# A recurrent attention kernel: small SBUF buffers laid out anew, and the score mask issued after the turn of q

## The chip, the cores and the metric

The kernel runs on one core of one Trainium2 chip. The metric is the device time of one execution in microseconds; three runs of the kernel before gave 2310.14, 2313.74 and 2330.06 us, so the median is 2313.74 us. Core engines are named as in the profile: PE (TensorE, matmuls; PEld is its weight load), DVE (VectorE), ACT (ScalarE), POOL (GpSimd) and SP (SyncE, which here only issues transfers). "L807" is line 807 of the kernel.

## The reference

Two branches work on the same 2048 tokens of width 1024 and are mixed by a sigmoid gate. The feed-forward branch is `gelu(x @ w_gate) * (x @ w_up) @ w_down`. The attention branch is a recurrence over 64 segments of 32 tokens; 8 memory rows go from each segment to the next:

```python
for s in range(n_seg):
    h = concatenate([mem, x[:, 32*s : 32*s+32]])      # 40 rows
    q, k, v = h @ Wq, h @ Wk, h @ Wv                  # 32 heads of 128
    scores = q k^T * scale, masked where idx >= M and key > query
    o = softmax(scores) v
    o = einsum('bhte,hed->btd', o, Wo)
    mem = o[:, :8]
    outs.append(o[:, 8:])
```

The next segment can't begin before `o[:, :8]` is there, and every segment needs all four weight matrices of 8 MB each, which don't all fit into SBUF.

## The kernel before, in words

**The rows.** Each segment is 40 rows: 8 of memory and 32 tokens. Only 24 of the tokens and the 8 memory rows (32 rows) go through the products with the fresh `h` (tile hT, [128, 8, 32], two of them, taken by turns: hT0 for even segments, hT1 for odd ones). The other 8 tokens of a segment don't depend on the memory as inputs, so their q, k and v are made ahead for four segments at once, from hR. This is called a fill (L836): eight products into one PSUM bank, a copy by ACT into a staging tile (fill_evac, L860), and for q and k a transpose on PE, a copy by DVE in place and a store to the DRAM scratch qk_scr (fill_put, L871); v is stored straight to v_scr. They are loaded back a segment at a time into qkr (load_qk, L542) and vB (load_v, L548).

**A segment.** The heads are taken in two halves, u = 0 and 1; r = 0 is the half that a segment does first (r = u exclusive-or the parity of s). Each of the products k, q, v and o is eight pieces (n = 0 to 7) for each half, four matmuls of 32 output rows on the four column groups of the array per piece. `walk` (L330) writes the order out: k 0 to 3, q 0 and 1 (r = 0), the last four pieces of the previous segment's o (r = 1), q 2 and 3, v 0 to 3, k 4 to 7, q 4 to 7, v 4 to 7; then k, q (r = 1), o (r = 0), v (r = 1), and o 0 to 3 (r = 1). All else is hung into this order by `plan` (L903): `on(m, r, n, f)` runs f just before piece n of product m. So each engine's instruction order is the order in which plan and walk emit; engines run in that order, and waits come from the overlap of SBUF byte ranges (cells of 64 bytes) and PSUM banks that `_Prog` (L31) records.

**Steps that the change touches.** With k in a PSUM bank, ACT copies it to a staging tile (evac, L671), PE turns it (four 128x128 transposes, L678), DVE copies it into kT (trans, L685), and POOL adds the 8 made-ahead columns from qkr (put_rest, L882). q goes the same way into qT. scores (L694) is one PE operation: first a matmul that writes the mask into bank SS (L697), then 32 small matmuls that add the scores (L703); DVE and ACT make the softmax, which ends in tAB (L723, over qT's memory). attend (L725) multiplies with vA and vB; take (L750) copies the result to oT; rest_o (L756) has POOL gather the 8 made-ahead rows into oRc, which SP stores to o_scr (L985), for a product over all segments at the end. After the first four pieces of o (r = 1), fold (L815) adds two halves of the output on DVE (with a scratch tile, part, in between) into a_bf; next_mem (L822) turns the memory rows out of a_bf into the next hT. fold and next_mem come twice, for the two halves of the width. POOL stores a_bf to a_scr (L1003).

**Weights.** 50 slots in SBUF hold the pieces; most have a slot of their own, while pieces 0 and 1 of k and q, 0 to 4 of v and 0, 1, 4, 5 and 6 of o share a slot between the halves and are loaded anew in each segment, about 7 MB. SP issues each of these loads when PE is through with the piece that it overwrites (spent, L447); neighbours are joined into one load of 1 MB (load_two, L425). All loads by SP go through one queue (q1), hT's (load_h, L533) among them.

**Memory of the small buffers.** In order of address, with bytes per partition: hT0 512, vB 512, hT1 512, qkr 768, oRc 512, a_bf 512, kT 1280, qT 1024, oT 1280. Others lie over these: part (1024, two of them by turns) over the old hT and vB; vA over oT; the staging tiles kS over kT, qS over qT, oS over oT, and pS over oRc and a_bf. kS takes Wk's first half and a segment's first fill, oS the second fill (two of every four segments have two fills), pS Wk's second half.

Of the kernel before, what the change touches and what calls it, by code (L numbers as in the profile page):

```python
# [210 lines left out]
def bass_gated_mix__memory_aug_recurrent_mem_tr__geglu_ffn__prompt_kernel(  # L211
# [34 lines left out]
    with ExitStack() as es:  # L246
# [57 lines left out]
        assert a_bf.off == oRc.off + 512  # L304
        stage = {n: al(n + "S", [128, 512], at=t.off) for n, t in (("k", kT), ("q", qT), ("o", oT), ("p", oRc))}
# [360 lines left out]
        def dve_copy(o, i, rd, wr):  # L666
            op("dve", lambda e: e.tensor_copy(o, i), rd=rd, wr=wr)  # L667
# [26 lines left out]
        def scores(u):  # L694

            def f(e):
                e.matmul(PB[SS][:, 0:320].rearrange("p (a c) -> p a c", a=4), lhsT=ident[:, :],  # L697
                         rhs=mS[:, :].unsqueeze(1).to_broadcast([128, 4, 80]), start=True, stop=False, skip_group_check=True)
                for n, c in ((32, 0), (8, 40)):
                    for j in range(4):  # L700
                        for g in range(4):
                            x = 8 * (4 * j + g)
                            ins = e.matmul(PB[SS][32 * g:32 * g + n, j * 80 + c:j * 80 + c + LQ],  # L703
                                           lhsT=qT[:, j, g, :] if n == 32 else qkr[:, 2 * u, x:x + 8],
                                           rhs=kT[:, j, g, :], start=False, stop=True, skip_group_check=True)
                return ins
            op("pe", f, rd=[qT.r(), qkr.r(256 * u, 256 * u + 128), kT.r(), ident.r(), mS.r()], wr=[BK(SS)])
# [107 lines left out]
        def fold(s, b):  # L815
            lo, hi = slice(64 * b, 64 * b + 64), slice(64 - 64 * b, 128 - 64 * b)
            pt, cs = part[s % 2], slice(256 * b, 256 * b + 256)
            op("dve", lambda e: e.tensor_copy(pt[lo, :], PB[XO][hi, cs]), rd=[BK(XO)], wr=[pt.r()])  # L818
            op("dve", lambda e: e.tensor_tensor(out=a_bf[lo, :], in0=PB[XO][lo, cs], in1=pt[lo, :], op=ALU.add),
               rd=[BK(XO), pt.r()], wr=[a_bf.r()])  # L820
# [82 lines left out]
        def plan(s):  # L903
# [29 lines left out]
            if not last:  # L933
                on("k", 0, 4, lambda: load_h(s + 1))
# [9 lines left out]
            if s > 0:  # L944
                on("v", 0, 7, lambda: scores(ua))
# [3 lines left out]
            if s == 0:  # L949
                on("k", 1, 1, lambda: scores(ua))  # L950
                on("k", 1, 1, lambda: attend(ua))
                on("k", 1, 1, lambda: fill0("k", 1, B0, "k"))
                on("q", 1, 0, lambda: fill0("q", 1, B1, "q"))
                on("q", 1, 4, lambda: fill0("v", 1, B2, "k"))
                on("q", 1, 4, lambda: (load_qk(0, 1), load_v(0, slice(1, 2)), load_r(1) if NG > 1 else None))
            else:
                on("v", 0, 5, lambda: load_qk(s, 1))
            on(*(("q", 1, 1) if s else ("o", 0, 0)), lambda: evac(bank_of["k", 1], stage["p" if s else "k"], "act"))
            if s > 0:
                on("o", 0, 0, lambda: attend(ua, ((0, "dve"),), TT))  # L960
                on("o", 0, 0, lambda: evac(bank_of["q", 1], stage["q"], "act"))
                on("o", 0, 0, lambda: trans(kT, "p", A0))
                on("o", 0, 0, lambda: put_rest())
                on("o", 0, 0, lambda: take(((1, "act"), (2, "act"))))
                on("o", 0, 2, lambda: trans(qT, "q", SS))
                on("o", 0, 2, lambda: take(((3, "dve"),), TT))
                on("o", 0, 2, lambda: rest_o(ua))
                on("o", 0, 4, lambda: scores(ub))
            else:
                on("o", 0, 0, lambda: trans(kT, "k"))  # L970
                on("o", 0, 0, lambda: put_rest())
                on("o", 0, 0, lambda: evac(bank_of["q", 1], stage["q"], "act"))
                on("o", 0, 2, lambda: trans(qT, "q"))
                on("o", 0, 6, lambda: scores(ub))
# [38 lines left out]
        fold(NSEG - 1, 1)  # L1013
# [4 lines left out]
        for b in range(NBK):  # L1018
            rb = rbs[b % 2]
            for hf in range(2):  # L1020
# [9 lines left out]
                cp[("act", "dve")[hf]](rb[0:RB, hf * 512:hf * 512 + 512], PB[bk][0:RB, :], [BK(bk)], [rb.r(hf * 512, hf * 512 + 512)])  # L1030
# [143 lines left out]
```

## Time and profile before

| what | number |
|---|---|
| median of three runs | 2313.74 us |
| the profiled execution itself | 2317.11 us |
| its span, first to last instruction | 2315.3 us |
| mean granted TensorE clock | 0.986 |
| PE busy | 2130.5 us (92%) |
| DVE, ACT, POOL busy | 1028.5, 543.2, 433.0 us |
| moved by DMA | 638.35 MB, mean 276 GB/s |
| of it by SP's queue (q1) | 596.59 MB |

Busy times say how much of the span an engine worked. A wait names the engine or transfer that released an instruction and the idle time ahead of it; idle time of an engine counts only where it sets the end. The ends of matmuls are modelled, so where PE seems busy the distance from start to start tells more. For a transfer the profile gives the issue and the time to landing, in which waiting in the queue is counted. Segments stand in the trace as stretches between stores of oRc (SPq L985). The recurrence takes the span up to about 1665 us, the rest is the product for the made-ahead rows and the feed-forward branch.

### The profile page before, as it was taken

The page shows a single profiled execution, that of the slowest core. Times are in us where ns is not written, and L with a number is a line of the kernel's source. Part 1 is how long each engine was busy: PE and PEld are TensorE (multiplying, and loading weights), DVE is VectorE, ACT ScalarE, POOL GpSimd, SP SyncE. Part 2 cuts the span into 40 slices and gives each one's busy share as a digit, 9 for nine tenths or more (in the row PEclk, how much of TensorE's full clock was granted, in tenths as well). Part 3 has the DMA queues.
Part 4 walks back from the last instruction along what each step waited for, and adds up shares of the span by engine and source line. Part 5 has one row for each costly group of instructions (what it writes and reads, how often), then busy time and mean ns, then how long its engine had stood idle before and what let it go on. Part 6 is the DMA issues. An engine that isn't in the chain of part 4 may idle for free.

```text
span 2315.3 us, 74604 instructions
## 1 busy us (share of the span) xinstructions
PE 2130.5 (92%) x33852; PEld 1060.6 (46%) x33852; DVE 1028.5 (44%) x2440; ACT 543.2 (23%) x1111; POOL 433.0 (19%) x821
## 2 busy tenths in 40 slices
PE   4488999999999999999999999998899999999999
PEld 2244444444444444444454445444464444444444
DVE  3344444444444444444444444444315346163462
ACT  1122222222222222222222222222113123032130
POOL 4422222222222222222222222221100000000000
PEclk9799999999999999999999999999999999999999
DMA  9999999899898999989999899998964450803520
GB/s 373 353 306 333 333 338 348 305 337 333 314 336 319 328 340 324 345 323 334 347 327 349 310 335 345 320 331 319 340 201 159 137 163 10 285 25 117 178 88 19
DMA packets 251964, 638.35 MB, mean 276 GB/s; under 512 B 23256, under 2 KB 92120, under 8 KB 251648
## 3 DMA queue, kind: packets, MB, share of 16 engines
q1 hardware_dynamic: 227824, 596.59, 72.3%
q0 software_dynamic: 13888, 26.31, 3.8%
q10 hardware_dynamic: 9936, 10.69, 1.4%
q8 instruction: 266, 4.36, 0.7%
q14 instruction: 50, 0.41, 0.1%
HBM read 596.85 MB, written 36.63 MB: 274 GB/s over the span
## 4 chain that ended last, share of the span: by engine, by line
PE 66%; DMA 22%; DVE 4%; issue 4%; ACT 3%; POOL 1%; ACTq 0%; POOLq 0%; SPq 0%
PE pb L774 19%; PE pb L1075 15%; DMA sl<-in_A_Wv_dram 7%; PE pb L1129 5%; PE pb L807 5%; PE pb L844 5%; DMA qk_scr<-oS 4%; PE pb L790 4%; PE pb L681 3%; PE pb L1026 3%; PE pb L854 2%; DMA qkr<-qk_scr 2%; PE pb L1110 2%; DMA wall<-wo_scr 1%; DMA xr_scr<-xr 1%
## 5 line engine op out<-in xcount | busy, mean ns | idle before, releaser
L774 PE MATMUL pb<-sl,hT 128*32 128x512 bf16 x12288 | 771.9, 382 | 27.0 <-issue 19.4
L774 PEld LDWEIGHTS pb<-sl,hT 128*32 128x32 bf16 x12288 | 348.7, 97 | 310.5 <-issue 37.6
L844 PE MATMUL pb<-sl,hR 128*32 128x512 bf16 x3072 | 221.3, 390 | 2.4 <-issue 1.8
L1075 PE MATMUL pb<-xT,wg 128*128 128x512 bf16 x896 | 211.7, 379 | 0.7
L1075 PE MATMUL pb<-xT,wu 128*128 128x512 bf16 x896 | 211.7, 379 | 0.0
L807 PE MATMUL pb<-wall,oT 128*32 128x256 bf16 x4056 | 148.7, 274 | 17.8 <-DMA wall<-in_A_Wo_dram 7.0
L757 POOL COPY oRc<-oT 128x128 bf16<-128x128 bf16 x128 | 96.3, 752 | 361.7 <-DVE oT L667 360.2
L790 PE MATMUL pb<-wall,oT 128*32 128x512 bf16 x2048 | 153.2, 391 | 9.5 <-issue 6.2
L818 DVE COPY part<-pb 64x256 f32<-64x256 f32 x128 | 54.0, 422 | 235.3 <-PE pb L807 234.3
L664 ACT ACTIVATE kS<-pb 128x512 bf16<-128x512 f32 x127 | 75.8, 597 | 344.2 <-PE pb L774 322.4
L1129 PE MATMUL pb<-wd,GT 128*128 128x512 bf16 x672 | 146.3, 379 | 1.3 <-DMA wd<-in_B_w_down_dram 1.3
L711 ACT ACTIVATE E<-pb 128x320 bf16<-128x320 f32 x128 | 56.0, 438 | 371.6 <-DVE pb L710 371.6
L1083 ACT ACTIVATE s<-pb 128x512 f32<-128x512 f32 x112 | 66.8, 596 | 311.7 <-PE pb L1075 311.7
L1075 PEld LDWEIGHTS pb<-xT,wg 128*128 128x128 bf16 x896 | 87.2, 98 | 107.9 <-DVE GT L1091 3.7
L1075 PEld LDWEIGHTS pb<-xT,wu 128*128 128x128 bf16 x896 | 87.7, 98 | 105.7
L1084 DVE SCALAR_TENSOR_TENSOR tp<-s,pb 128x512 f32<-128x512 f32 x112 | 76.9, 687 | 124.2 <-ACT s L1083 124.0
L807 PEld LDWEIGHTS pb<-wall,oT 128*32 128x32 bf16 x4056 | 100.3, 96 | 67.6 <-ACT oT L664 26.1
L667 DVE CAST oT<-pb 128x160 bf16<-128x160 f32 x256 | 76.4, 320 | 115.2 <-PE pb L740 115.2
L667 DVE COPY kT<-pb 128x512 bf16<-128x512 bf16 x128 | 54.4, 425 | 158.1 <-PE pb L681 157.7
L664 ACT ACTIVATE vA<-pb 128x512 bf16<-128x512 f32 x128 | 76.2, 596 | 199.1 <-PE pb L774 151.7
L883 POOL COPY kT<-qkr 128x128 bf16<-128x128 bf16 x128 | 37.3, 292 | 431.2 <-DVE kT L667 272.5
L1088 DVE SCALAR_TENSOR_TENSOR tp<-tp,pb 128x512 f32<-128x512 f32 x112 | 77.0, 687 | 78.5 <-ACT tp L1087 78.5
(93 smaller groups left out, 2283.1 us busy)
## 6 DMA issues: line engine op xcount, KB each, us to landing
sl<-in_A_Wv_dram SPq DMA_DIRECT2D x128, 1024.0 KB, 11.2
wall<-wo_scr SPq DMA_DIRECT2D x175, 512.0 KB, 6.3
sl<-in_A_Wk_dram SPq DMA_DIRECT2D x64, 1024.0 KB, 5.8
sl<-in_A_Wq_dram SPq DMA_DIRECT2D x64, 1024.0 KB, 9.3
wall<-wo_scr SPq DMA_DIRECT2D x55, 1024.0 KB, 8.4
wd<-in_B_w_down_dram SPq DMA_DIRECT2D x42, 1024.0 KB, 5.6
sl<-in_A_Wv_dram SPq DMA_DIRECT2D x75, 512.0 KB, 11.6
wall<-in_A_Wo_dram SPq DMA_DIRECT2D x41, 512.0 KB, 7.7
```

The costliest lines, as they stand in the source:

```text
L664: op("act", lambda e: e.activation(o, i, ACTF.Copy), rd=rd, wr=wr)
L667: op("dve", lambda e: e.tensor_copy(o, i), rd=rd, wr=wr)
L681: ins = e.transpose(PBV[bank][:, j * 128:(j + 1) * 128], st[:, j * 128:(j + 1) * 128], ident[:, :])
L757: op("pool", lambda e: e.tensor_copy(oRc[:, :, 16 * u:16 * u + 16].rearrange("p c x -> p x c"), oT[:, :, :, 32:40].rearrange("p g j c -> p ...
L774: ins = e.matmul(PB[bk][32 * g:32 * g + 32, :], lhsT=h[:, i, :], rhs=w[:, g * 512:(g + 1) * 512], start=(n == 0), stop=(n == 7))
L790: ins = e.matmul(PB[XO][32 * g:32 * g + 32, :], lhsT=oT[:, j, x, 0:32], rhs=wall[:, na:nb + 1:nb - na, c:c + 256], start=(n == 0 and hp == 0),
L807: ins = e.matmul(PB[XO][32 * g:32 * g + 32, 256 * b:256 * b + 256], lhsT=oT[:, j, x, 0:32], rhs=w[:, c:c + 256], start=False, stop=(n % 4 ...
L844: ins = e.matmul(PB[b][32 * g:32 * g + 32, :], lhsT=h[:, k[2], :], rhs=w[:, g * 512:(g + 1) * 512], start=(n == 0), stop=(n == 7))
L1075: ins = e.matmul(PB[bk][:, 0:FB], lhsT=w[:, kc, cc:cc + 128], rhs=xT[:, :, :, kc, :].rearrange("p t i c -> p (t i) c"), start=(kc == 0), s ...
L1084: op("dve", lambda e, hg=hg, t=t: e.scalar_tensor_tensor(out=t[:, :], in0=s1[:, :], scalar=1.0, in1=hg, op0=ALU.add, op1=ALU.mult), rd=[BK ...
L1088: op("dve", lambda e, hu=hu, t=t: e.scalar_tensor_tensor(out=t[:, :], in0=t[:, :], scalar=1.0, in1=hu, op0=ALU.add, op1=ALU.mult), rd=[BK( ...
L1129: ins = e.matmul(PB[bank[2 * k + hf]][:, :], lhsT=GT[:, j, tb * 128:(tb + 1) * 128], rhs=w[:, jj, hf * 512:(hf + 1) * 512], start=(j == 0) ...
```

## The change

The layout becomes hT0, oRc, hT1, qkr, vB, a_bf, kT, qT, oT. part is one tile over qT. Two staging tiles of 1024 bytes replace pS and the use of oS in the recurrence: stage 0 is hT0 and oRc, stage 1 is oRc and hT1. In segment s the fill's second store and Wk's second half both use the stage with the hT of the previous segment. So load_h(s + 1), which writes that hT, moves from before k 4 to after the turn of Wk's second half at o 0 (r = 0). fill_evac of the second fill moves from before q 2 to the end of the steps at k 0, fill_put from before v 3 to before q 2 (behind fold). load_v moves from behind fold(s, 1) to before o 2 (r = 1). The mask matmul becomes an operation of its own, issued right after the turn of q; the second q's turn uses bank A1 instead of SS, so that SS is free for the mask. `ended` adds one wait in the last product, since part now lies where that product's result is copied.

```diff
         hT0 = al("hT0", [128, KC, 32])
+        oRc = al("oRc", [128, NB, 32])
+        hT1 = al("hT1", [128, KC, 32])
+        assert oRc.off == hT0.off + 512 and hT1.off == oRc.off + 512
+        hT = (hT0, hT1)
+        qkr = al("qkr", [128, 3, 128])
         vB = al("vB", [128, 2, 128])
-        hT1 = al("hT1", [128, KC, 32])
-        assert vB.off == hT0.off + 512 and hT1.off == vB.off + 512
-        hT = (hT0, hT1)
-        part = tuple(al(f"part{n}", [128, 256], FP32, at=o) for n, o in enumerate((hT0.off, vB.off)))
-        qkr = al("qkr", [128, 3, 128])
-        oRc = al("oRc", [128, NB, 32])
         a_bf = al("a_bf", [128, 256])
...
-        assert a_bf.off == oRc.off + 512
-        stage = {n: al(n + "S", [128, 512], at=t.off) for n, t in (("k", kT), ("q", qT), ("o", oT), ("p", oRc))}
+        part = al("part", [128, 256], FP32, at=qT.off)
+        stage = {n: al(f"{n}S", [128, 512], at=t.off) for n, t in (("k", kT), ("q", qT), ("o", oT), (0, hT0), (1, oRc))}
...
-        def scores(u):
+        def mask():
+            op("pe", lambda e: e.matmul(PB[SS][:, 0:320].rearrange("p (a c) -> p a c", a=4), lhsT=ident[:, :],
+                                        rhs=mS[:, :].unsqueeze(1).to_broadcast([128, 4, 80]), start=True, stop=False,
+                                        skip_group_check=True), rd=[ident.r(), mS.r()], wr=[BK(SS)])
+
+        def scores(u, masked=True):
+            if not masked:
+                mask()
...
-            if not last:
+            if not last and s == 0:
                 on("k", 0, 4, lambda: load_h(s + 1))
...
             on("v", 0, 5 if s else 6, lambda: trans(qT, "q", A0 if s else TT))
             if s > 0:
+                on("v", 0, 5, mask)
                 on("v", 0, 7, lambda: scores(ua))
...
-            on(*(("q", 1, 1) if s else ("o", 0, 0)), lambda: evac(bank_of["k", 1], stage["p" if s else "k"], "act"))
+            on(*(("q", 1, 1) if s else ("o", 0, 0)), lambda: evac(bank_of["k", 1], stage[ub if s else "k"], "act"))
             if s > 0:
                 on("o", 0, 0, lambda: attend(ua, ((0, "dve"),), TT))
                 on("o", 0, 0, lambda: evac(bank_of["q", 1], stage["q"], "act"))
-                on("o", 0, 0, lambda: trans(kT, "p", A0))
+                on("o", 0, 0, lambda: trans(kT, ub, A0))
+                if not last:
+                    on("o", 0, 0, lambda: load_h(s + 1))
                 on("o", 0, 0, lambda: put_rest())
                 on("o", 0, 0, lambda: take(((1, "act"), (2, "act"))))
-                on("o", 0, 2, lambda: trans(qT, "q", SS))
+                on("o", 0, 2, lambda: trans(qT, "q", A1))
+                on("o", 0, 2, mask)
                 on("o", 0, 2, lambda: take(((3, "dve"),), TT))
                 on("o", 0, 2, lambda: rest_o(ua))
                 on("o", 0, 4, lambda: scores(ub))
...
             if two:
-                on("q", 0, 2, lambda: fill_evac(*fl[1], B0, "o"), **nx)
+                on("k", 0, 0, lambda: fill_evac(*fl[1], B0, ua), **nx)
             on("q", 0, 2, lambda: fold(s, 1), **nx)
-            on("q", 0, 2, lambda: load_v(s + 1), **nx)
+            if two:
+                on("q", 0, 2, lambda: fill_put(*fl[1], ua, SS), **nx)
+            on("o", 1, 2, lambda: load_v(s + 1))
             on("v", 0, 3, lambda: next_mem(s, 1), **nx)
-            if two:
-                on("v", 0, 3, lambda: fill_put(*fl[1], "o", SS), **nx)
...
-                cp[("act", "dve")[hf]](rb[0:RB, hf * 512:hf * 512 + 512], PB[bk][0:RB, :], [BK(bk)], [rb.r(hf * 512, hf * 512 + 512)])
+                cp[("act", "dve")[hf]](rb[0:RB, hf * 512:hf * 512 + 512], PB[bk][0:RB, :], [BK(bk)], [rb.r(hf * 512, hf * 512 + 512)],
+                                       *([[ended]] if hf and b < 2 else []))
```

More of the change, by code (lines that the diff above doesn't have):

```diff
@@ L664, in act_copy, with dve_copy @@
             op("act", lambda e: e.activation(o, i, ACTF.Copy), rd=rd, wr=wr)
-        def dve_copy(o, i, rd, wr):
-            op("dve", lambda e: e.tensor_copy(o, i), rd=rd, wr=wr)
+        def dve_copy(o, i, rd, wr, after=()):
+            op("dve", lambda e: e.tensor_copy(o, i), rd=rd, wr=wr, after=after)
         cp = {"act": act_copy, "dve": dve_copy}
@@ L706, in f @@
                 return ins
-            op("pe", f, rd=[qT.r(), qkr.r(256 * u, 256 * u + 128), kT.r(), ident.r(), mS.r()], wr=[BK(SS)])
+            op("pe", f, rd=[qT.r(), qkr.r(256 * u, 256 * u + 128), kT.r()], wr=[BK(SS)])
             op("pool", lambda e: e.memset(pAB[:, 256:544].bitcast(FP32), 0.0), wr=[pAB.r(256)])
@@ L816, in fold @@
             lo, hi = slice(64 * b, 64 * b + 64), slice(64 - 64 * b, 128 - 64 * b)
-            pt, cs = part[s % 2], slice(256 * b, 256 * b + 256)
+            pt, cs = part, slice(256 * b, 256 * b + 256)
             op("dve", lambda e: e.tensor_copy(pt[lo, :], PB[XO][hi, cs]), rd=[BK(XO)], wr=[pt.r()])
-            op("dve", lambda e: e.tensor_tensor(out=a_bf[lo, :], in0=PB[XO][lo, cs], in1=pt[lo, :], op=ALU.add),
+            return op("dve", lambda e: e.tensor_tensor(out=a_bf[lo, :], in0=PB[XO][lo, cs], in1=pt[lo, :], op=ALU.add),
                rd=[BK(XO), pt.r()], wr=[a_bf.r()])
@@ L949, in plan @@
             if s == 0:
-                on("k", 1, 1, lambda: scores(ua))
+                on("k", 1, 1, lambda: scores(ua, False))
                 on("k", 1, 1, lambda: attend(ua))
@@ L973, in plan @@
                 on("o", 0, 2, lambda: trans(qT, "q"))
-                on("o", 0, 6, lambda: scores(ub))
+                on("o", 0, 6, lambda: scores(ub, False))
             on("v", 1, 0, some(f1, 3))
@@ L1012, in bass_gated_mix__memory_aug_recurrent_mem_tr__geglu_ffn__prompt_kernel @@
         fold(NSEG - 1, 0)
-        fold(NSEG - 1, 1)
+        ended = fold(NSEG - 1, 1)
         op("pool", lambda e: e.dma_start(a_scr[NSEG - 1].rearrange("g r c -> (g r) c"), a_bf[:, :]), rd=[a_bf.r()],
```

2 lines of the change are left out of this document (removed).

## The prediction

> **What bounds the kernel now.** I read the page first (TensorE 92% busy, DMA at nine tenths), then the sums by stage, because the recurrence and the feed-forward part have different limits, then the waits, then the order of time of one segment.
>
> ```profile
> 1000.00:1300.00 300.00, 285.86 (x6086) 147.37 (x6086) 144.14 (x396) 78.22 (x174) 77.05 (x154) 1.00 0.94 340
> 1014.73:1039.07 24.34, 23.18 (x497) 12.02 (x498) 11.72 (x32) 6.43 (x14) 5.68 (x11) 1.00 0.93 332
> 1700.00:2315.30 615.30, 610.26 (x2847) 283.36 (x2845) 275.69 (x405) 139.18 (x227) 0.00 (x0) 1.00 0.38 122
> ```
>
> The columns are the stretch, its length, busy PE, PEld, DVE, ACT, POOL, the granted clock, the DMA share and GB/s. The change lies wholly in the recurrence (about 90 to 1665 us, 64 segments of some 24.3 us; the second row is one of them, from one store of oRc to the next). There PE is busy 95% of the time and the DMA engines 93 to 94%: two resources near their limit at once, so a wait that goes on one side is worth only what the other side lets through. The last 615 us are untouched.
>
> ```profile
> ACT vA L664 <- DMA qk_scr<-oS: 47.4, 24, 2.9
> PE pb L732 <- ACT vA L664: 17.3, 24, 1.5
> PEld pb L774 <- DMA sl<-in_A_Wv_dram: 20.2, 31, 1.8
> PEld pb L697 <- DVE qT L667: 53.1, 112, 0.9
> PE pb L697 <- POOL kT L883: 6.9, 9, 1.1
> PEld pb L681 <- ACT pS L664: 10.1, 32, 1.3
> ```
>
> Each row of the waits: who waited, for what, total us, times, longest. The first two are the stall that the new layout is about: half of the segments store a second fill from oS, which is oT's and vA's memory, so vA's copy waits for that store and PE's attend (L732) waits for vA. The third names the other limit: in 31 segments PE's weights for the last Wv pieces come only just from the DMA.
>
> ```profile
> 1022.20 0.77 POOL L879 DMA_DIRECT2D qk_scr<-oS  x1 [0.57 <-DVE oS L876]
> 1029.68 0.60 ACT L664 ACTIVATE vA<-pb 128x512 bf16<-128x512 f32 x1 [2.17 <-PE pb L774]
> 1030.17 0.59 ACT L664 ACTIVATE pS<-pb 128x512 bf16<-128x512 f32 x1
> 1030.33 0.27 PE L732 MATMUL pb<-tAB,vA 32*128 32x40 bf16 x16 [0.73 <-ACT vA L664]
> 1030.82 0.40 PE L681 MATMUL pb<-ident,pS 128*128 128x128 bf16 x4
> 1082.85 0.40 PE L774 MATMUL pb<-sl,hT 128*32 128x512 bf16 x4 [0.29 <-DMA sl<-in_A_Wv_dram]
> ```
>
> Here is the one kind of segment (PE idle 0.73 us for vA at 1030) and the other (PE idle for Wv at 1082).
>
> ```profile
> 1017.98 0.38 SPq L436 DMA_DIRECT2D sl<-in_A_Wk_dram  x1
> 1022.23 0.49 SPq L535 DMA_DIRECT2D hT<-xq_scr  x1
> 1024.20 0.34 SPq L381 DMA_DIRECT2D sl<-in_A_Wv_dram  x1
> sl<-in_A_Wv_dram SPq DMA_DIRECT2D x75, 512.0 KB, 11.6
> hT<-xq_scr SPq DMA_DIRECT2D x63, 64.0 KB, 12.2
> vB<-v_scr POOLq DMA_DIRECT2D x63, 64.0 KB, 6.6
> qk_scr<-oS POOLq DMA_DIRECT2D x31, 128.0 KB, 7.2
> o_scr<-oRc SPq DMA_DIRECT2D x64, 64.0 KB, 3.9
> 1018.00:1020.00 2.00, 2.00 (x59) 1.46 (x55) 0.09 (x1) 0.09 (x1) 0.00 (x0) 1.00 0.39 96
> 1030.00:1032.00 2.00, 1.57 (x36) 0.85 (x36) 0.75 (x2) 1.75 (x5) 0.26 (x1) 1.00 1.03 408
> ```
>
> A transfer of 64 KB that takes 12.2 us is a transfer that queues. SP's queue is issued from 1017.98 on, the engines stand at 0.39 around 1019 and at 1.03 at 1031, and the last Wv piece, issued at 1024.20, lands some 11.6 us later, at 1035.8. So each segment is a loop of two parts: a transfer stretch from Wk's issue to the last Wv's landing (1035.8 - 1018.0 = 17.8 us), then a PE chain (last v product, attend, half an output product, fold, new memory rows) to the next issue of Wk (24.3 - 17.8 = 6.5). PE's work inside the first part counts only where PE is later than the Wv landing.
>
> **The change part by part.**
>
> *Second fill staged in the old hT beside oRc.* The store no longer holds vA. What is late next: the DVE chain into tAB, which ends (row below) at 1028.89 + 0.77 = 1029.66, against a start of L732 at 1030.33.
>
> ```profile
> 1028.89 0.77 DVE L723 STREAM_TRANSPOSE tAB<-pAB 128x256 bf16<-128x256 bf16 x2
> ```
>
> So nearly all of the 0.73 us goes there, and the 17.3 us over the 24 waits is the price. It counts only where Wv is not later: 63 - 31 = 32 segments of 63, so 17.3 x 32/63 = 8.8 us. Bounds: 0 (all lost to Wv) and 17.3.
>
> *Wk's second half staged there too, not in oRc and a_bf.* Its copy no longer waits for a_scr's store, but for the second fill's. That store stands five products earlier in PE's order (20 matmuls of 56 ns by the rows of the next part, 1.1 us), of which I count 0.7, because fold's second step stays ahead of it on DVE; so it is issued at 1021.5 and lands near 1021.5 + 7.2 = 1028.7; the copy (0.60) is done at 1029.3, before PE's turn of it (1030.82 now, about 1030.1 then). The waits for pS are 10.1 us on PEld over 32 times; I take a fifth, 2.1 us, since in the order of time they lie mostly behind running matmuls. Bounds 0 and 10.1.
>
> *The mask follows the turn of q.* Same matmul, put where PE waits for DVE's copy of qT.
>
> ```profile
> 1000.15 0.40 PE L681 MATMUL pb<-ident,qS 128*128 128x128 bf16 x4
> 1000.48 0.61 PE L774 MATMUL pb<-sl,hT 128*32 128x512 bf16 x8
> 1000.58 0.42 DVE L667 COPY qT<-pb 128x512 bf16<-128x512 bf16 x1 [0.35 <-PE pb L681]
> 1001.07 0.31 PE L697 MATMUL pb<-mS,ident 128*128 128x320 bf16 x1
> 1001.31 0.28 PE L703 MATMUL pb<-kT,qT 128*32 128x40 bf16 x16
> 1095.77 3.87 PE L774 MATMUL pb<-sl,hT 128*32 128x512 bf16 x68
> 1099.57 0.53 PE L732 MATMUL pb<-tAB,vA 32*128 32x40 bf16 x16
> ```
>
> Read starts, not busy time: 68 products take 1099.57 - 1095.77 = 3.80 us, 56 ns each, so the eight from 1000.48 are through at 1000.93, and the mask waits for qT (1001.00) until 1001.07. It then takes 0.24 us to the first score. With the mask first, the scores start at 1000.48 + 0.24 + 0.45 = 1001.17 instead of 1001.31: 0.14, say 0.15 us. Two a segment, in the 32 segments where PE counts: 32 x 0.30 = 9.6 us. Bounds: 0 (no loss, since PE does the same work in another order), and 126 x 0.24 = 30 if every mask fell into a wait. A1 as q's bank instead of the score bank is what makes this possible; its next writer, the first fill, comes 2 us after DVE has read it, so I cost that at nothing.
>
> *load_h moved from k's middle to after the turn of Wk's second half, load_v from behind fold to o's second half.* Both leave the transfer stretch: hT stood in SP's queue ahead of the last Wv piece, vB among the transfers beside Wq. 64 KB at 408 GB/s is 0.16 us each. vB leaves the stretch wholly only in the half of the segments without v stores ahead of it on POOL's queue: 0.16 + 0.08 = 0.24 us, in the 31 segments where Wv is the limit 7.4 us. Bounds: 0 and 63 x 0.32 = 20. On SP the new load_h waits for PE's turn; behind it come only the wall loads, which need later PE work, so they lose nothing but its issue (0.49 us), for which there is room (below: from 1031.2 to 1031.81). It then lands behind the last Wv, about 1035.8 + 0.2 = 1036; DVE writes the memory rows into it at 1040.33. Cover 4 us. Upper bound by the row of now: 12.2 us after 1031.2, 1043.4, which would cost 3.1 us x 63 = 195 us; I take 1036, because at 1031 the queue holds nothing issued after 1024.20.
>
> ```profile
> 1031.81 1.20 SPq L379 DMA_DIRECT2D wall<-wo_scr  x2
> 1040.33 0.17 DVE L831 COPY hT<-pb 128x32 bf16<-128x32 bf16 x1 [0.32 <-PE pb L828]
> 1014.73 0.32 SPq L985 DMA_DIRECT2D o_scr<-oRc  x1
> 1039.07 0.32 SPq L985 DMA_DIRECT2D o_scr<-oRc  x1
> 1018.62 1.14 PE L807 MATMUL pb<-wall,oT 128*32 128x256 bf16 x31
> 1042.39 1.05 PE L807 MATMUL pb<-wall,oT 128*32 128x256 bf16 x32
> ```
>
> [...]
>
> *New wait: the second fill's copy needs oRc, so the store of oRc must have landed.* Behind it on ACT stands k's copy, twenty products later, but PE's turn of that fill now stands right after the last output products. Store 1014.73 + 3.9 = 1018.6, copy 0.60, 1019.2; PE is there at about 1019.7: free. In the other kind of segment 1039.07 + 3.9 + 0.6 = 1043.6 against 1042.39 + 1.05 = 1043.4: 0.2 late, and some 0.2 more because vB now runs beside it: 0.4 us x 15 segments = 6, of which half counts (PE's part of the stretch): 3 us lost. Bounds 0 and 15 x 0.8 = 12. DVE's copies beyond fold change places at equal length; the last `ended` wait is one instruction.
>
> Sum: 8.8 + 2.1 + 9.6 + 7.4 - 3 = 24.9 us less. The profiled execution took 2317.1 us (span 2315.3), 3.4 above the median of the runs, 2313.7; so 2292 for such an execution and 2289 for the median.
>
> **The rivals.**
>
> *Transfers hide the gain (chance 0.18).* If the Wv landing binds nearly everywhere once PE is faster, only the transfers' 0.24 us x 31 = 7.4 stay: 2306. For it: 31 waits for Wv, DMA share 0.94. Against: 24 waits for vA with PE truly idle, and 0.39 around 1019. The Trainium skill, DMA: Bandwidth & Descriptors, Specifications, puts a core's HBM limit near 358 GB/s, by which 340 GB/s would leave 5% at most and this rival would be likelier; the trace disagrees, with 408 GB/s over two microseconds.
>
> *Everything counts (0.15).* 17.3 + 19 (126 x 0.15) + 6.9 (kT's wait, passed by the mask) + 2.1 = 45: 2268. For it: less PE lateness also issues Wk earlier. Against: the Wv waits.
>
> *The store of oRc holds PE (0.07), slower.* The turn of the second fill waits at q's third product. It decides from a landing 4.3 us after issue; at 6 us it costs (6 - 4.3) x 31 = 53, less the 25 gained: 2342. For it: vB and hT now run nearer to it. Against: median 3.9.
>
> *hT comes late (0.04), slower.* From 4 us later than I reckon; each further us costs 63: about 2350.
>
> **How the numbers follow.** My forecast, 2289, has 0.56, with a spread of 2277 to 2302 by the bounds of its terms. About 1% (23 us, below 2290.6 or above 2336.9) is what a measurement of this kernel can tell from no change. Faster: a little over half of the forecast's share, 0.31, and the third case, 0.15: 0.46. Same: 0.25 + 0.18 and 0.01 of the slower ones: 0.44. Slower: 0.10. The range, 2268 to 2314, takes in the second and third case and leaves out the slower ones and a little at the lower end.
>
> **What would show it.** Right: no wait of vA for a qk_scr store; scores starting about 0.15 us sooner after q's turn; hT landing within 6 us of its issue; segments ending on Wv's landing more often than 31 times. Wrong: PE idle at L681 ahead of q's third product with ACT or the o_scr store as releaser; L831 waiting for hT's load; SP's wall loads issued later after the turn of Wk; or the segment no shorter although vA's wait is gone.

## The result and the profile after

The change made the kernel 0.3% faster: 2309.57 us, the median of 20 runs (2303.76 to 2319.04), against 2315.16 of 20 runs of the kernel before; ratio 0.9971, interval 0.996 to 0.9981. That is 5.6 us less. The forecast was 24.9 us less, so the direction was right and the size was not. The profiled execution took 2311.04 us (span 2309.2), 6.1 us below that of before. Every ratio below is to runs of the kernel before that were taken with the run in question; executions of one kernel lie up to 27 us apart.

Shown of the kernel after: one stretch of the recurrence (columns as in the prediction), then the rows of the transfers that the change moved, each with its count, its size and the median time from issue to landing.

```profile
1000.00:1300.00 300.00, 280.48 (x6019) 143.06 (x6011) 141.89 (x390) 76.30 (x170) 75.33 (x153) 1.00 0.94 336
```

```profile
sl<-in_A_Wv_dram SPq DMA_DIRECT2D x75, 512.0 KB, 11.0
...
o_scr<-oRc SPq DMA_DIRECT2D x64, 64.0 KB, 4.3
...
hT<-xq_scr SPq DMA_DIRECT2D x63, 64.0 KB, 5.4
...
vB<-v_scr POOLq DMA_DIRECT2D x63, 64.0 KB, 4.4
```

The DMA share is 0.94 as before. hT lands in 5.4 us where it took 12.2, vB in 4.4 instead of 6.6, the last Wv pieces in 11.0 instead of 11.6, and the store of oRc in 4.3 instead of 3.9. The transfers did what the prediction said of them.

The waits of the kernel after (who waited, for what, total us, times, longest). The one on which the old layout's stall rested, ACT's copy into vA behind the store of the second fill, is gone; the rows that stand in its place are these. 0S and 1S are the two new staging tiles.

```profile
ACT 0S L663 <- DMA o_scr<-oRc: 37.8, 8, 5.0
...
ACT 1S L663 <- DMA o_scr<-oRc: 35.6, 7, 8.4
...
PEld pb L778 <- DMA sl<-in_A_Wv_dram: 21.0, 25, 2.2
...
PE pb L778 <- issue: 19.4, 24, 1.9
...
PE pb L811 <- issue: 13.7, 17, 2.0
...
PE pb L794 <- issue: 11.2, 9, 2.7
...
PE pb L707 <- issue: 7.5, 14, 1.5
PE pb L707 <- POOL kT L887: 7.2, 13, 1.4
...
PE pb L736 <- ACT vA L663: 3.0, 4, 0.8
```

PE's wait for vA (last row) fell from 17.3 to 3.0 us. ACT waits for the store of oRc 15 times (first two rows), the new wait that the prediction named. PE's weights wait for the last Wv piece 25 times, where it was 31. In the four rows with "issue" PE waits for nothing that the profile shows. The same rows of the kernel before were smaller for both halves of o (L807, L790) and for the scores:

```profile
PE pb L774 <- issue: 19.4, 22, 2.5
...
PE pb L807 <- issue: 6.9, 12, 1.1
...
PE pb L790 <- issue: 6.2, 6, 2.7
...
PE pb L703 <- issue: 3.9, 8, 1.2
```

To see where the time went I took the starts of the same PE instructions in each of segments 12 to 62 (51 segments that all do the same loads, each cut where the last v product of a segment starts) and summed the distances between them. Four stretches hold the PE instructions that the change moves and the wait that it takes away; "the rest" is everything else. The last row sums PE's idle time that the profile puts to "issue" in these segments. A two-fill segment is one in which a second fill is copied and turned; there are 24 among these. Us over the 51 segments, one profiled execution each:

| stretch, from and to PE's start of | before | after |
|---|---|---|
| v's fifth product, first scores (mask) | 82.0 | 69.6 |
| o's first piece (r = 0), second scores (mask) | 103.5 | 91.1 |
| q's first piece (r = 1), attend (vA) | 108.7 | 98.1 |
| o's fifth piece (r = 1), k's fifth product (turn of the second fill) | 138.7 | 149.0 |
| the rest | 801.9 | 824.3 |
| all | 1234.9 | 1232.2 |
| of it waits for "issue" | 35.8 | 53.8 |

(The other 3.4 us of the 6.1 between the two executions lie outside these segments.) So the four stretches together gave 25.1 us. And 22.4 of them came back in the rest, where the change moves no PE instruction, 18.0 by the measure of the "issue" waits. Where the segments are cut matters a little: cut at each segment's first k product, the sums are 1234.8 and 1229.5, and 19.8 came back. The granted clock did not take the gain: between 400 and 1600 us it was 1.00, 1.00 and 0.99 by thirds in the kernel before, and 1.00 in all three in the kernel after. The experiments ask what did.

### The profile page after: what moved, and what is told of

It is laid out like the page before. It is cut to its first block, busy times and chain, and to the rows that moved or that the text cites. A ratio compares the mean times of both kernels' runs of the same rounds, so it can differ in the third digit from the quotient of the medians.

```text
span 2309.2 us, 74637 instructions
## 1 busy us (share of the span) xinstructions
PE 2112.1 (91%) x33852; PEld 1044.8 (45%) x33852; DVE 1028.6 (45%) x2440; ACT 541.3 (23%) x1111; POOL 423.7 (18%) x821
## 4 chain that ended last, share of the span: by engine, by line
PE 69%; DMA 19%; issue 4%; DVE 4%; ACT 2%; POOL 1%; ACTq 0%; SPq 0%; POOLq 0%
PE pb L778 23%; PE pb L1084 15%; DMA sl<-in_A_Wv_dram 7%; PE pb L1138 6%; PE pb L811 4%; PE pb L848 4%; PE pb L794 4%; PE pb L680 3%; PE pb L1034 2%; DMA wall<-wo_scr 2%; DMA qkr<-qk_scr 2%; PE pb L1119 2%; PE pb L858 2%; DMA o_scr<-oRc 1%; DMA xr_scr<-xr 1%
## 5 line engine op out<-in xcount | busy, mean ns | idle before, releaser
L778 PEld LDWEIGHTS pb<-sl,hT 128*32 128x32 bf16 x12288 | 336.4, 97 | 333.8 <-issue 52.5
L794 PE MATMUL pb<-wall,oT 128*32 128x512 bf16 x2048 | 151.9, 385 | 20.0 <-issue 11.2
```

Source lines behind the costliest of these rows:

```text
L778: ins = e.matmul(PB[bk][32 * g:32 * g + 32, :], lhsT=h[:, i, :], rhs=w[:, g * 512:(g + 1) * 512], start=(n == 0), stop=(n == 7))
L794: ins = e.matmul(PB[XO][32 * g:32 * g + 32, :], lhsT=oT[:, j, x, 0:32], rhs=wall[:, na:nb + 1:nb - na, c:c + 256], start=(n == 0 and hp == 0),
```

## The experiments

Three theories of the give-back stand in the expectations where letters are used. W: the landing of Wv's last pieces sets the end of a segment, so PE's gain is capped there (the prediction's own rule). F: PE's instruction transfers are what PE waits for, so their number matters. D: the load on the DMA engines as a whole returns the gain, through every wait that a transfer ends, those of PE's own instructions among them. Against all three stands luck: where PE's instructions happen to lie. Three more letters appear there: S, the gain went into the new wait for the store of oRc; G, the "issue" waits belong to PE's own order, whatever the transfers do; C, the granted clock falls without the warming matmuls.

**The parts alone.** First the layout without the mask's move, then the mask's move on the old layout.

```diff
# e1_mask_late, on the kernel after
-                on("v", 0, 5, mask)
-                on("v", 0, 7, lambda: scores(ua))
+                on("v", 0, 7, lambda: scores(ua, False))
-                on("o", 0, 2, mask)
-                on("o", 0, 4, lambda: scores(ub))
+                on("o", 0, 4, lambda: scores(ub, False))
...
# e2_mask_only, on the kernel before
+                on("v", 0, 5, mask)
-                on("o", 0, 2, lambda: trans(qT, "q", SS))
+                on("o", 0, 2, lambda: trans(qT, "q", A1))
+                on("o", 0, 2, mask)
...                       (and mask() taken out of scores(), as in the change)
```

> The changed kernel with the mask put back ahead of the scores, all else of the change kept. In the changed kernel's trace the mask's move saves 0.24 us at each of the two scores of a segment, some 25 us over segments 12 to 62 and 31 over all 64, while waits named issue ahead of PE's instructions grew by 18 us. Theory F (the saved time is given back to PE's waits for its own instruction fetch, the 16 KB transfers of the instruction queue): only part of the 31 us comes back as time, 5 to 18 us more than the changed kernel, 2315 to 2328, and the issue waits fall from about 66 to 50. Theory S (the gain went into the new wait for the store of oRc and the mask counts in full): about 31 us more, 2340. Theory W (the landing of the last Wv piece sets each segment's end, PE's work does not count): no difference, 2310.

> The kernel before with the mask's move alone (the second q turned in bank A1, the mask behind each turn). Theory F: 3 to 12 us less than the kernel before, with issue waits up from about 42 to 50 or more. Theory S: 25 to 31 us less, since the store wait is not there. Theory W: no difference.

Measured: 1.0008 (0.9988 to 1.0027) for the layout alone and 1.0007 (0.9991 to 1.0023) for the mask alone. Neither shows a gain by itself. In the mask's run the two score stretches shrank from 82.0 to 69.9 and from 103.5 to 89.5 us, 26.1 in all, but the stretch that ends at attend grew by 7.0: the store that vA waits for lands when it did, and PE is only there sooner. The rest grew by 18.0. In the layout's run vA's stretch fell by 12.8, the turn's grew by 9.8, and the rest grew by 20.0. So a give-back comes with either part. That of the layout's run is the less certain: its profiled execution (2328.42 us) was 8.5 above the median of its runs, and its granted clock by the same thirds was 0.98, 1.00 and 0.99.

**The moved turn of the second fill, and the store of oRc.** The fill stays in the old hT, but is copied and turned at its old places; and, apart from that, the store of oRc goes to POOL's queue, right behind rest_o.

```diff
# e3_fill_old_place, on the kernel after
-                on("k", 0, 0, lambda: fill_evac(*fl[1], B0, ua), **nx)
+                on("q", 0, 2, lambda: fill_evac(*fl[1], B0, ua), **nx)
...
-            if two:
-                on("q", 0, 2, lambda: fill_put(*fl[1], ua, SS), **nx)
...
             on("v", 0, 3, lambda: next_mem(s, 1), **nx)
+            if two:
+                on("v", 0, 3, lambda: fill_put(*fl[1], ua, SS), **nx)
# e4_store_pool, on the kernel after: moved to right behind attend(ub)
-            on("o", 1, 0, lambda: op("sp", lambda e: e.dma_start(o_scr[s], ...
+            on("o", 1, 0, lambda: op("pool", lambda e: e.dma_start(o_scr[s], ...
```

> The changed kernel with the second fill's copy and turn at their old places (copy ahead of q's third product, turn ahead of v's fourth), still staged in the old hT beside oRc. The o_scr store has then landed when ACT copies, and the 0.2 to 0.3 us of PE's wait ahead of q's third product in the two-fill segments go, some 8 to 10 us in all. Theory S: at least 10 us less than the changed kernel, up to 20: 2290 to 2300. Theory F: 2 to 8 us less, the rest given back to issue waits. Theory W: no difference. If the later store of the fill then holds Wk's copy, PE's turn of Wk would wait for ACT, and the time could be longer than the changed kernel's by a few us.

> The changed kernel with the store of oRc issued by POOL right behind its copy into oRc, not by SP behind the wall and qkr loads. If its landing is late because it stands behind SP's loads, it lands sooner than the 4.3 us of the changed kernel, about 3.3 as the fill's store of the same stretch does, and the wait of ACT for it is gone from PE's path. Theory S: 8 us or more less than the changed kernel. Theory F: 0 to 6 us less. Theory W: no difference. POOL's issue takes about 0.5 us each; nothing on POOL is due in that stretch, so it should cost nothing.

With the old places: 2306.66 us, 0.9958 (0.994 to 0.9977), the fastest kernel of this study that computes everything; its interval overlaps that of the change as made (0.996 to 0.9981), so the two are not told apart. The stretch of the turn fell from 149.0 to 142.8 us, and the sum of the segments by 6.5 (1232.2 to 1225.7).

Why the moved turn costs is seen in the order of time of the kernel after, at one of its two-fill segments:

```profile
1134.60 0.40 PE L680 MATMUL pb<-ident,1S 128*128 128x128 bf16 x4
1135.15 0.43 DVE L823 TENSOR_TENSOR a_bf<-pb,part 64x256 bf16<-64x256 f32 x1
1135.61 0.42 DVE L880 COPY 1S<-pb 128x512 bf16<-128x512 bf16 x1
1136.12 0.11 PEld L832 LDWEIGHTS pb<-ident,a_bf 64*128 64x128 bf16 x2 [0.42 <-DVE 1S L880]
1136.39 0.17 DVE L835 COPY hT<-pb 128x32 bf16<-128x32 bf16 x1 [0.35 <-PE pb L832]
1136.62 0.55 PEld L778 LDWEIGHTS pb<-sl,hT 128*32 128x32 bf16 x16 [0.23 <-DVE hT L835]
```

PE's four transposes of the fill (L680) used to stand between next_mem's turn (L832) and the product that reads hT, so they covered DVE's copy into hT. Now they stand earlier, and that product waits for the copy (last row). The counts of that wait say the same: some 30 more with the moved turn, one for each second fill, and none more with the old places (before, after, old places):

```profile
PEld pb L774 <- DVE hT L831: 14.7, 65, 0.3
PEld pb L778 <- DVE hT L835: 21.5, 94, 0.2
PEld pb L778 <- DVE hT L835: 14.5, 64, 0.3
```

The store by POOL's queue was expected to remove the other half of that stretch. It did not: 1.0019 (0.9999 to 1.004), and the stretch stayed at 150.1 us. The store landed only a little sooner (last row below), and ACT waited for it 22 times instead of 15. ACT also came to wait for the v stores of the fills, which POOL issues behind it on the same queue, and PE for ACT's copy:

```profile
ACT kS L663 <- DMA v_scr<-kS: 100.8, 11, 11.2
...
PE pb L680 <- ACT kS L663: 35.4, 13, 6.6
```

```profile
o_scr<-oRc POOLq DMA_DIRECT2D x64, 64.0 KB, 3.9
```

In the kernel after these two waits were

```profile
ACT kS L663 <- DMA v_scr<-kS: 9.3, 2, 4.7
...
PE pb L680 <- ACT kS L663: 18.5, 5, 6.1
```

ACT's 100.8 us count its whole idle time before these copies. What counts is PE's wait: after 380 us it comes nine times in this run, 0.3 to 3.2 us each and 19.8 in all, and never in the kernel after. The v stores take no longer to land (3.5 us at the median, against 3.6), but POOL issues them 2.2 us behind ACT's copy instead of 1.4; whether that alone makes the wait is not shown. The expectation that the issue on POOL "should cost nothing" was wrong, and since the run has this cost of its own, it does not price the store of oRc.

**Without the transfers.** In both kernels all reloads of weights are left out from segment 12 on.

```diff
# e5_after_no_reload, e6_before_no_reload, in spent
             done[n] += 1
+            if now[0] >= 12:          # the segment
+                return
```

> The changed kernel with all reloads of weight pieces left out from segment 12 on (about 7 MB of each segment's 8 MB of transfers), so that the output is not the reference's; PE, ACT, DVE and POOL do the same instructions. Theory F (issue waits are PE waiting for its instruction transfers, which queue behind the weight transfers): the issue waits of segments 12 to 62, 53.8 us in the changed kernel, fall below 8. Rival G (they are something of PE's own order, independent of the DMA load): they stay at 40 or more. By F those segments take 1232 less 54, less some 25 of other DMA waits and late stores, 1150 us; theory W would give the same fall without the issue waits changing.

> The kernel before with the same reloads left out from segment 12 on (output not the reference's). With the DMA engines nearly idle the store from oS should land in 3 us and the wait of vA for it be gone without the new layout. Theory F: issue waits below 8 us here too, and what is left between the two kernels is the mask's move alone, 25 us in segments 12 to 62 (30 in all), with nothing given back. If the two differ by less than 10 us, the mask's gain is lost to something other than transfers.

Measured: 2197.07 us, 0.9481 (0.9435 to 0.9526), and 2219.55 us, 0.9578 (0.9533 to 0.9623). The change is worth 22.5 us here, four times what it is worth under the full load. The same stretch of time in the changed kernel without reloads, and all rows of its PE waits that name "issue" and come to more than 0.5 us, over its whole span:

```profile
1000.00:1300.00 300.00, 296.30 (x6487) 154.43 (x6475) 150.83 (x417) 81.31 (x181) 81.91 (x166) 1.00 0.12 30
```

```profile
PE pb L782 <- issue: 2.6, 4, 1.0
...
PE pb L798 <- issue: 1.4, 1, 1.4
PE pb L684 <- issue: 1.1, 1, 1.1
...
PE pb L815 <- issue: 0.6, 2, 0.3
```

With the DMA share down from 0.94 to 0.12, the "issue" waits of segments 12 to 62 are 0.3 us (0.2 in the kernel before). So the reloads make them. By stretches:

| | before, no reloads | after, no reloads |
|---|---|---|
| the two score stretches | 168.5 | 143.9 |
| to attend | 94.8 | 94.5 |
| the turn's | 135.5 | 140.9 |
| the rest | 747.6 | 749.1 |
| all | 1146.4 | 1128.4 |

Three things are read here. The mask saves its whole 24.6 us. The vA wait is no gain, since the store lands early without the load; under load it gave 10.6. And the moved turn costs 5.4 us with no reload to blame, 0.22 in each of the 24 two-fill segments. Of the 10.3 under load 8.9 lie in these segments, so at most 3.5 are left there for the store of oRc. PE's own waits for ACT's copies into the two staging tiles, which that store can hold up, are smaller still, over the whole span of the kernel after:

```profile
PE pb L680 <- ACT 0S L663: 1.8, 6, 0.5
...
PE pb L680 <- ACT 1S L663: 0.9, 4, 0.3
```

In the row "the rest" of the table, 1.5 comes back instead of 22.4.

**Luck of placing.** 64 tiny matmuls (128 PE instructions with their weight loads) ahead of the first segment shift where PE's instructions lie.

```diff
# e7_after_pad, e8_before_pad
+        def pad(e):
+            for _ in range(64):
+                ins = e.matmul(PB[B2][:, 0:8], lhsT=ident[:, :], rhs=ident[:, 0:8], start=True, stop=True)
+            return ins
+        op("pe", pad, rd=[ident.r()], wr=[BK(B2)])
         load_h(0, "pool")
```

> The changed kernel with 64 tiny matmuls (128 PE instructions, half of the 256 that one 16 KB instruction transfer holds) added in the start-up, where PE is idle, so that the instruction transfers' borders fall half a transfer away in every segment. Theory F with luck of placing (the 18 us more of issue waits in the changed kernel come from where the borders happen to fall): issue waits of segments 12 to 62 move by 10 us or more from 53.8, and the time by 5 us or more. Theory F without luck (PE runs out of instructions more often because it waits less elsewhere): issue waits within 8 us of 53.8 and the time within 4 us of 2310.

> The kernel before with the same 64 tiny matmuls. With luck of placing: its issue waits (35.8 us in segments 12 to 62) move by 10 us or more and the time by 5 us or more, and the padded kernels may stand the other way round. Without: issue waits within 8 us of 35.8, the time within 4 us of 2316, and the changed kernel with the pad still has 10 us more of issue waits than this.

Measured: 0.9996 (0.9977 to 1.0015) and 1.0014 (0.999 to 1.0039). The "issue" waits stay where they were, 52.2 us with the order of after and 31.0 with that of before, and so does the rest, 820.9 and 796.1. So the larger waits of the new order outlast this one shift, which speaks against luck.

**Fewer PE instructions.** The warming matmuls, which only keep PE busy while the memory rows are made, are left out: with the fill's turn at its old places, and on the kernel after.

```diff
# e9_fill_old_no_warm (with the edits of e3), e10_after_no_warm; the same for warm(5)
-            on("k", 0, 0, some(f2, 4) if two else lambda: warm(2), **nx)
+            on("k", 0, 0, some(f2, 4), **nx)
...
```

> The changed kernel with the second fill's copy and turn at their old places (as in the earlier run) and without the 28 warming matmuls (56 PE instructions of about 1010) that the segments without a second fill issue around fold. The warming products fill a stretch in which PE waits for DVE's fold anyway, but each counts for the instruction transfers. Theory F: PE waits there idle and its instruction transfers catch up; issue waits of segments 12 to 62 fall from 49.4 us to 40 or less, most of it between the first half of the output product and the next k (0.58 and 0.13 us a segment in the changed kernel where no second fill stands), and the time falls to 2295 to 2304, below both kernels. Rival (PE's work as such is what counts there): the same phase gets shorter without the issue waits elsewhere changing, 3 us at most. Rival C: the granted clock falls without the warming products, and the time rises.

> The changed kernel without the warming products, all else of it kept. Theory F: issue waits of segments 12 to 62 fall from 53.8 us to 45 or less, and the time by 3 to 10 us from the changed kernel's; against the run with the fill at its old places too it is 3 to 8 us longer, since the new place costs PE 6 us. Rival C: longer, with a lower granted clock.

Measured: 1.0013 (0.9989 to 1.0037) and 1.0024 (1.0011 to 1.0037): no gain. Against e3 and the kernel after, "issue" fell by some ten us (49.4 to 38.8, and 53.8 to 44.0), yet the time went up: PE stands idle for the memory rows, where the warming had stood (first row), and the scores wait longer for POOL's columns of kT (second row),

```profile
PE pb L832 <- DVE a_bf L823: 36.0, 42, 1.1
...
PE pb L707 <- POOL kT L887: 24.0, 29, 2.0
```

(the run on the kernel after, where these two waits were 2.5 and 7.2 us). The granted clock was 0.99 from 400 us on, against 1.00 in the kernel after, and may have a part in it. So F does not hold as put: the ten us taken from one wait did not reach the end. As the edit brings waits of its own, it does not refute that these waits cost time.

**A little less load.** The last reloaded piece of Wv (0.5 MB of some 7 in a segment) is left out from segment 12 on.

```diff
# e11_after_less_wv, e12_before_less_wv, in spent
             done[n] += 1
+            if now[0] >= 12 and k[0] == "v" and k[2] == 4:
+                return
```

> The changed kernel with one of the fourteen reloaded pieces of a segment (the last of Wv, 0.5 MB of about 8 MB) left out from segment 12 on, so that the output is not the reference's. It takes 1.3 us of the DMA engines' time in a segment of 24.1. Without any reload the changed kernel's segments 12 to 62 are 104 us shorter and those of the kernel before 88 us. Theory D (the transfers as a whole set the pace: PE time that is saved comes back as a wait for one transfer or another, the instruction transfers most): 25 to 55 us less than the changed kernel, 2255 to 2285, and issue waits down from 53.8 to 45 or less. Theory F alone (only the instruction transfers' queueing counts, whatever the volume): less than 12 us, issue waits above 48. Theory W (only the landing of that last piece counts): 25 us or more less, with the issue waits unchanged.

> The kernel before with the same piece's reload left out. Theory D: 20 to 45 us less than the kernel before, and the two kernels now differ by more than the 5.6 us of the full load, by 8 to 18 us, because PE counts for more when the transfers have room. Theory F alone: less than 12 us less, the same difference as before.

Measured: 2296.75 us, 0.9901 (0.9874 to 0.9928), and 2318.62 us, 0.9983 (0.9962 to 1.0004). The second is the sharper one. In the kernel before, v's second half (from the start of its first product to that of its last) shrank from 96.5 to 80.6 us, and in no segment does v's last product start within 0.06 us of Wv's landing any more (20 of 51 before). Still the time did not move: all of the 15.9 us were given back, 11.2 of them between the start of o's first piece of the second half and the next k. So in the order of before, Wv's landing is not what sets the end, and W falls there. In the kernel after, v's second half shrank by 17.8 us and 10.2 of them reached the sum of the segments (1232.2 to 1222.0); there this run cannot part W from D, since the edit brings both a sooner landing and a lighter load.

D's sizes for the two runs were too large as well, and the "issue" waits did not fall to 45: they were 51.4 in the kernel after, and 41.0 in the kernel before, more than its 35.8 under the full load. But D's sign for the difference held. The change is worth 0.9901/0.9983, 0.8% or about 19 us, with this piece out. The four stretches gave 29.9 us and 11.7 came back, against 25.1 and 22.4 with it.

## Why the prediction was right and wrong

(The forecast's terms are for 63 segments, the measured stretches for 51.)

*The wait for vA* (8.8 us): right in its mechanism and within its bounds. It went, 10.6 us in 51 segments. Without the reloads it is worth nothing.

*Wk's second half* (2.1 us): no row of the trace parts its gain from the rest, so it stays open.

*The mask* (9.6 us): mis-sized. It was priced at 0.15 us in half of the segments. It gave its full 0.24 us at the first scores (82.0 less 69.6 over 51 is 0.24) and as much at the second, on the mean of all segments: 24.8 us, where the stated upper bound for 63 segments was 30. The sum from the rows was short because it let the mask begin where the products had begun, 0.33 us after q's turn (1000.15 to 1000.48 in the prediction's rows). In the kernel after the mask begins 0.23 us after it:

```profile
1019.36 0.40 PE L680 MATMUL pb<-ident,qS 128*128 128x128 bf16 x4
1019.59 0.30 PE L694 MATMUL pb<-mS,ident 128*128 128x320 bf16 x1
1019.82 0.61 PE L778 MATMUL pb<-sl,hT 128*32 128x512 bf16 x8
1020.27 0.28 PE L707 MATMUL pb<-kT,qT 128*32 128x40 bf16 x16
```

From the turn to the scores it is 0.91 us here and was 1.16.

*The moved transfers* (7.4 us): the mechanism was right and its worth was not. The stretch from Wk's issue to Wv's landing became shorter, on the mean by 0.25 to 0.54 us depending on the kind of segment (17.54 to 17.00 at best). But v's last product started within 0.06 us of that landing in 13 segments of 51 instead of 20, where "more often than 31 times" was the sign given for right, and in the order of before, the run without a Wv piece shows that a sooner landing moves no time.

*The new wait for the store of oRc* (3 us lost): at most 3.5 in the 24 two-fill segments, and PE's waits for ACT's copies into the staging tiles come to 2.7 over the whole span. So the size was about right; no run shows the store's part by itself.

*"DVE's copies beyond fold change places at equal length"* was wrong. The copies are of equal length; but PE's turn of the fill was the cover of DVE's copy into hT, and moving it cost 5.4 us.

*The step that failed* is the rule by which these terms were added: "It counts only where Wv is not later: 63 - 31 = 32 segments of 63". It named one transfer as the cap and put every other wait that could take the gain back at nothing, the wait for PE's own instructions among them. The touched stretches gave 25.1 us in 51 segments, about 31 at that rate in 63, so that their nearness to the 24.9 of the forecast is luck. The cap lay elsewhere: 22.4 us came back in the rest, in stretches of o, v and the scores' neighbours that the change leaves alone. Shown: without reloads 1.5 came back, with 0.5 MB less 11.7, with all of them 22.4, and two orders shifted by a pad kept their own waits. So the load on the DMA engines takes the gain, and the largest part of it by the measure of the waits (18.0 us) as idle time of PE with no releaser. The rival "transfers hide the gain" came nearest with 2306, but by the wrong transfer, and that is luck too.

What those "issue" waits are is read from one of the longest in the kernel after, first PE's order of time, then the queues of a stretch in it (packets, MB, share of the engines):

```profile
855.49 1.05 PE L794 MATMUL pb<-wall,oT 128*32 128x512 bf16 x15
859.21 0.38 PE L794 MATMUL pb<-wall,oT 128*32 128x512 bf16 x1 [2.67 <-issue]
```

```profile
q1 hardware_dynamic: 268, 0.56, 98.8%
q8 instruction: 1, 0.02, 4.5%
```

PE stops in the middle of an output product whose weights and inputs are there, and a 16 KB transfer of the instruction queue falls in the pause, among 268 packets of SP's queue that fill 98.8% of the engines. In both kernels every "issue" wait of PE over 0.25 us between 400 and 1660 us (42 in the kernel before, 53 in that after) stands beside the start of such a transfer; nearly always PE goes on about 2.4 us after that start, and the instructions where it does lie multiples of 256 apart (to within two, weight loads counted), at the same places of both kernels' order. There are 266 of these transfers in either, one for every 256 of the 68190 instructions of PE. So the waits are for PE's instructions.

That these transfers begin late can be read by putting them beside the borders, the places 256 instructions apart: the first transfer beside the first border, and so on. In segments 12 to 62 (192 transfers) a transfer begins at the median 3.4 us after PE has passed its border in the kernel before and 3.6 in the kernel after. Without the reloads it is 0.4 and 0.5 us. PE comes to the next border about 6.4 us on (1232.2 / 192), and where it waits there, it goes on some 2.4 us after the transfer's start; so a start at 3.6 us is still in time. The slowest quarter (3.9 and 4.0 us and more) hardly is, and 42 and 53 waits on some 196 transfers between 400 and 1660 us are about a quarter. By this working an order that needs less time for its 256 instructions has to wait more often, as the kernel after does.

The Trainium skill, Runtime: NRT & Kernel Launch, Instruction fetch mechanics, says that the sequencer fetches blocks of 16 KiB, 256 instructions, by its own DMA queue, and calls the cost of crossing a border "mostly hidden". The trace agrees on the 256, and disagrees on hidden at a DMA share of 0.94: 53.8 us of waits in 51 segments, up to 2.67 us each. At 0.12 it agrees, with 0.3.

Still open: behind which packets a block's transfer stands. That the reloads delay its start by some 3 us is measured; that it queues behind SP's packets is argued from that. Open too is why the "issue" waits of the kernel before rose when 0.5 MB were left out. Open is also why 18 us come back already with the mask alone (its touched stretches gave 16.2), that is, what amount of give-back belongs to which transfer, and 4.4 of the 22.4 us have no "issue" wait to show for them. Each sum by stretches rests on one profiled execution, and executions of one kernel differ by up to 27 us; the runs that carry the argument agree among themselves (the rest is 796 to 803 us in three kernels with the order of before and 814 to 824 in three with that of after).

## What to carry to other kernels

Where two resources are both above nine tenths, price a saving on one by a run with the other relieved: it shows the saving's own worth (22.5 us here) and so what the other takes back. Before moving an instruction, ask which wait it covers where it stands; here four transposes hid a copy. Sum the waits for "issue" too: where they go when the load on the DMA engines is taken away, as here from 53.8 to 0.3 us, the transfers make them.

## What the runs showed of the hardware

PE's waits for its instructions came to 0.2 and 0.3 us in 51 segments at a DMA share of 0.12 and to 31.0 to 53.8 under the full load, by the order of work; with 0.5 MB a segment less, at a share of 0.88 and 0.89, they were 41.0 and 51.4, so they do not follow the load in small steps. A transfer of 16 KB in the instruction queue takes 1.0 us at the median under the full load and 1.1 without it. So it is not slower; it starts some 3 us later. And the store of 64 KB landed at the median in 3.9 us on POOL's queue and 4.3 on SP's under the full load, against 2.3 on SP's without the reloads: here the load set the time far more than the queue did.
